# Two large tiles for v instead of three, and the last batch's v in the buffers of q and k

## The chip, the cores and the metric

The kernel runs on one core of one Trainium2 chip. The metric is the device time of one execution in microseconds (us). The kernel before took 256.08 us, the median of 3 runs (256.04 to 256.36).

## The reference

Two stages are computed for 4 batches of 6400 rows with 256 channels. The first is a cross-covariance attention: q and k are normalised along the rows, s = kn^T qn is a 256 x 256 matrix per batch, a is its softmax, and the result is v a. The second is a mixture of adapters: a gate picks 2 of 8 experts for each row and adds their low-rank (16) updates.

```python
qn = q / (np.linalg.norm(q, axis=1, keepdims=True) + 1e-06)
kn = k / (np.linalg.norm(k, axis=1, keepdims=True) + 1e-06)
s = kn.transpose(0, 2, 1) @ qn / tau
a = softmax(s)                      # over the last axis
x = (v @ a).reshape(25600, 256)
logits = x @ w_gate                 # 8 experts
topk = the two largest logits       # w: their softmax
out = x + sum over the two experts e of w_e * ((x @ A[e]) @ B[e])
```

The statistics of a batch need all of its q and k; only then can the rows of its v be worked on. q, k and v are float32 in memory, 26.2 MB each, and so is the output.

## The kernel before, in words

The 6400 rows of a batch lie on 128 partitions, 50 rows on each. A *chunk* is one such row index on all partitions (128 x 256 elements), so a batch has 50 chunks of each of q, k and v. A *pair* is two chunks of v and the unit of the second half of the work: pairs 0 to 24 belong to batch 0, 25 to 49 to batch 1, 50 to 74 to batch 2, 75 to 99 to batch 3.

**Loads.** All loads but the first few go through GpSimd's queue (POOL, lines 148, 149 and 151), which turns float32 into bf16 on the way. q and k come in tiles of 10 chunks each (one tile holds both; four buffers), v in tiles of 18, 16 and 16 chunks per batch (`VP`, three buffers). The list `loads` is sorted by the pair at which each load is due; `load_more` issues them strictly in that order and stops at the first one whose buffer still has unused chunks. So a load that waits for its buffer holds up all loads behind it. Since transposes wait for the load that holds their chunks, a load is of use only when the whole of it has landed. Batch 0's v and the last tile of v come in smaller pieces.

**Batch 0 first.** A first loop runs over batch 0's q and k: squares (ScalarE and VectorE in turn, lines 241 and 243), the Gram matrix on TensorE (`gram`, line 251), and sums of squares (`norm`). Then `chain0` to `chain6` turn them into the softmax matrix and its product with the gate's weights and the first adapter matrices.

**The slot loop.** After that a loop goes through slots. In slot n TensorE transposes pair n of v (`transposes`, line 400), and works on earlier pairs: `z_gz` (line 506), `gz_t` (line 530), `y_mm` (line 522), `delta` (line 542), and ScalarE copies the result into a buffer `ys` (line 546). Every five pairs form a group, with logits (line 421), a gating chain on VectorE, and one output of 10 chunks (1.31 MB). Into the same slots the Gram matrix of the next batch is dealt: batch 1 in slots 0 to 20, batch 2 in 24 to 45, batch 3 in 49 to 67, each followed by its chain. Each engine executes its instructions in the order in which this loop writes them.

**Outputs.** There are nine `ys` buffers. A finished group is put on the list `unsent`, and `send` (line 563, issued by ScalarE) sends groups only while more than `keep` are held: 7 until slot 70, then one less every four slots. The last ten pairs go out in small pieces by SyncE (line 550).

Of the kernel before, what the change touches and what calls it, by code (L numbers as in the profile page):

```python
# [9 lines left out]
BF16 = mybir.dt.bfloat16  # L10
# [6 lines left out]
def kernel(  # L17
# [17 lines left out]
    B, N, C = q.shape  # L35
    P = 128
# [8 lines left out]
    PC = 10  # L45
    NPAIR = NC // 2
    NPT = B * NPAIR
    GRP = 5
    QKB, VB, YB = 4, 3, 9
    VP = [18, 16, 16]  # L50
    FIRST = 4
    DEFER = 7

    GRAM = {1: (0, 20), 2: (24, 45), 3: (49, 67)}
# [9 lines left out]
    v_pool = ctx.enter_context(tc.tile_pool(name="vp", bufs=VB))  # L64
# [19 lines left out]
    for b, (first, last) in GRAM.items():  # L84
        n = last - first + 1
        for c in range(NC):
            s = first + c * n // NC
# [4 lines left out]
    loads = []  # L92

    for s in range(NC // PC):
        o = FIRST if s == 0 else 0
# [1 line left out]
        for b in range(1, B):  # L97
            loads.append((qk_need[b, s], "qk", b, s, 0, [PC]))
    for b in range(B):
        for s, n in enumerate(VP):  # L100
            at = NPAIR * b + sum(VP[:s]) // 2 + 1
            if b == 0:

                loads.append((at, "v", b, s, 0, [n - 8]))
                loads.append((at + (n - 8) // 2, "v", b, s, n - 8, [8]))
            else:
                loads.append((at, "v", b, s, 0,
                              [8, 4, 4] if b == B - 1 and s == len(VP) - 1 else [n]))
    loads.sort(key=lambda x: x[0])
    tiles = {"qk": {}, "v": {}}  # L110
    left = {"qk": [], "v": []}
    bufs = {"qk": QKB, "v": VB}
    where = {}
    at_load = [0]

    def piece(kind, c):

        if kind == "qk":
            return divmod(c, PC)
        s = 0  # L120
        while c >= VP[s]:
            c -= VP[s]
            s += 1
        return s, c

    def used(kind, b, c, n):
        left[kind][where[kind, b, piece(kind, c)[0]]] -= n

    def load_more(limit=1000):

        while limit and at_load[0] < len(loads):
            _, kind, b, s, o, parts = loads[at_load[0]]
            if (kind, b, s) not in where:
                n = len(left[kind])
                if n >= bufs[kind] and left[kind][n - bufs[kind]]:
                    return
                where[kind, b, s] = n
                left[kind].append(PC if kind == "qk" else VP[s])
                if kind == "qk":
                    t = qk_pool.tile([P, 2, PC, C], BF16, tag="qk", name="qk")  # L140
                else:
                    t = v_pool.tile([P, max(VP), C], BF16, tag="v", name="vt")
                tiles[kind][b, s] = t
            t = tiles[kind][b, s]
            c0 = s * PC if kind == "qk" else sum(VP[:s])
            for m in parts:
                if kind == "qk":
                    nc.gpsimd.dma_start(t[:, 0, o:o + m, :], q_v[b, :, c0 + o:c0 + o + m, :])  # L148
                    nc.gpsimd.dma_start(t[:, 1, o:o + m, :], k_v[b, :, c0 + o:c0 + o + m, :])
                else:  # L150
                    nc.gpsimd.dma_start(t[:, o:o + m, :], v_v[b, :, c0 + o:c0 + o + m, :])  # L151
                o += m
            at_load[0] += 1
            limit -= 1
# [22 lines left out]
    for c in range(0, FIRST, 2):  # L177
        t = tiles["qk"][0, 0]
# [54 lines left out]
    def square(b, c, eng):  # L233

        s, o = divmod(c, PC)
        t = tiles["qk"][b, s]
        sq = sq_pool.tile([P, 2, 2, C], BF16, tag="sq", name="sq")
        sqs[b, c] = sq
        src = t[:, :, o:o + 2, :]
        if eng == "act":  # L240
            nc.scalar.activation(sq, src, ACT.Square)  # L241
        else:
            nc.vector.tensor_tensor(out=sq, in0=src, in1=src, op=OP.mult)  # L243
# [137 lines left out]
    pr = {}  # L381
    free_banks = [False]
    unsent = []

    LAST = {NPT - 9: 4, NPT - 7: 4, NPT - 6: 2, NPT - 4: 4, NPT - 3: 2, NPT - 2: 2, NPT - 1: 2}

    def transposes(g, eng):

        b, p = divmod(g, NPAIR)
        gr = groups[g]  # L390
        if "vT" not in gr:
            gr["vT"] = vt_pool.tile([P, CC, 2 * GRP, P], BF16, tag="vT", name="vT")
        s, o = piece("v", 2 * p)
        vt = tiles["v"][b, s]
        full = ps_t.tile([P, 512], FP32, tag="pt", name="vT_ps")
        pt = full[:, 0:256].bitcast(BF16).rearrange("p (c t) -> p c t", c=CC)
        i = 0
        for sc in range(2):
            for ic in range(CC):
                nc.tensor.matmul(pt[:, ic, sc * P:(sc + 1) * P],  # L400
                                 vt[:, o + sc, ic * P:(ic + 1) * P], ident,
                                 is_transpose=True, start=(i == 0), stop=(i == 3))
                i += 1
        used("v", b, 2 * p, 2)
        w = 2 * (g - gr["f"])
        dst = gr["vT"][:, :, w:w + 2, :]
        src = pt.rearrange("p c (s t) -> p c s t", s=2)
        if eng == "act":
            nc.scalar.copy(dst, src)  # L409
        else:  # L410
            nc.vector.tensor_copy(dst, src)  # L411
        gr["full"] = full
        pr[g] = {"vT": dst, "w": w}
# [82 lines left out]
    def z_gz(u):  # L496
        b = u // NPAIR
        r, gr = pr[u], groups[u]

        banks = [(ps_z, "zg"), (ps_z, "zg"), (ps_acc, "acc"), (ps_nrm, "nrm")]  # L500
        pool, tag = banks[u % 4 if free_banks[0] else 0]
        zg = pool.tile([P, 512], FP32, tag=tag, name="zg")
        z = zg[:, 0:256].rearrange("p (s d) -> p s d", s=2)
        for sc in range(2):
            for ic in range(CC):
                nc.tensor.matmul(z[:, sc, :], r["vT"][:, ic, sc, :], st[b]["wa"][:, ic, E:E + ER],  # L506
                                 start=(sc == 0 and ic == 0), stop=(sc == 1 and ic == 1),
                                 skip_group_check=True)
        gz = work.tile([P, 2, ER], BF16, tag="gz", name="gz")
        nc.vector.tensor_tensor(  # L510
            out=gz.rearrange("p c (e r) -> p c e r", e=E),
            in0=z.rearrange("p c (e r) -> p c e r", e=E),
            in1=gr["gate"][:, r["w"]:r["w"] + 2, :].to_broadcast([P, 2, E, R]), op=OP.mult)
        r["gz"], r["zg"] = gz, zg
# [41 lines left out]
    def send(keep):  # L556


        eng = nc.scalar
        while len(unsent) > keep:  # L560
            gr = unsent.pop(0)
            c0, n = 2 * (gr["f"] - gr["b"] * NPAIR), 2 * gr["n"]
            eng.dma_start(out_v[gr["b"], :, c0:c0 + n, :], gr["ys"][:, 0:n, :])
# [49 lines left out]
    slot = 0  # L613
    zq, dq = None, None
    while nz < NPT or zq is not None or dq is not None:

        behind = nz + GRP < min(slot, NPT) and groups[nz + GRP]["ready"]
        items = [] if behind else todo.get(slot, [])
        h = (len(items) + 1) // 2
        f, us, fb = (None, 0.0, 0) if behind else at_chain.get(slot, (None, 0.0, 0))  # L620
        free_banks[0] = slot > GRAM[B - 1][1] + 4
        load_more()
        for b, c in items:
            if c % 2 == 0:
                square(b, c, "act")
        if f in (chain0, chain1, chain2, chain3):
            f(fb)
        u = None
        if nz < min(slot, NPT) and groups[nz]["ready"]:
            u = nz  # L630
            nz += 1
            z_gz(u)
        if zq is not None:
            gz_t(zq, "act" if slot >= NPT else "dve")
        gram_part(items[:h])
        if dq is not None:
            y_mm(dq)
        if slot < NPT and not behind:
            transposes(slot, "dve" if items or f is chain3 else "act")
        if dq is not None:  # L640
            delta(dq)
        dq, zq = zq, u
        send(max(0, min(DEFER, DEFER - (slot - GRAM[B - 1][1]) // 4)))
        if behind:
            deal(0.3)
            continue
        if 0 < slot <= NPT and slot - 1 == groups[slot - 1]["f"] + groups[slot - 1]["n"] - 1:
            logits(groups[slot - 1])
            ops = gating(groups[slot - 1])
            credit[0] -= ops[0][0]  # L650
            ops[0][1]()
            micro += ops[1:]
        gram_part(items[h:])
        if f in (chain4, chain5, chain6):
            f(fb)
        if items:
            deal(max(0.8 - us, 0.6))
        elif slot < NPT:
            deal(max(0.65 - us, 0.4))
        else:  # L660
            deal(0.5)
        slot += 1
# [35 lines left out]
```

## Time and profile before

| what | value |
|---|---|
| median of 3 runs | 256.08 us (256.04 to 256.36) |
| the profiled execution's own time | 255.97 us |
| its span, from the first to the last event in the profile | 254.2 us |
| TensorE (PE) busy | 220.1 us, 87% of the span |
| ScalarE (ACT) busy | 176.7 us, 70% |
| VectorE (DVE) busy | 155.4 us, 61% |
| GpSimd (POOL) busy | 32.6 us, 13% |
| loads through POOL's queue | 38.80 MB written in bf16, 59 issues |
| outputs by ScalarE, 1280 KB each | 18 issues, median 12.8 us from issue to landing |
| last output issued | 246.8 us |

The profile numbers lines by the file of its kernel (L400 is line 400), and times from the start of the span. A view in order of time has the start, the duration, the engine and line, the operation with its result and operands, and in brackets how long the engine stood idle just before and what ended that. In the view of the page's 40 slices each digit is the busy share of a slice of 6.4 us in tenths, and the row GB/s is what the transfers moved, counted in bytes as written: for a load that is half of what is read. A row of the view by stretches has the stretch, its length, the busy time and the number of instructions of PE, PEld (the weight loads), DVE, ACT and POOL, and then the TensorE clock that was granted, the share of the transfer engines and GB/s. A row of waits has the total, the number of times and the longest. A row of DMA issues has the queue, the number, the size as written and the median from issue to landing.

### The profile page before, as it was taken

Reading aid. Unit: us, or ns where it says so; the run is one execution under the profiler, and the core shown is the slowest. Engines: PE = TensorE matmul, PEld = TensorE weight load, DVE = VectorE, ACT = ScalarE, POOL = GpSimd, SP = SyncE. Lnnn points to the kernel's source line nnn. Section 1 sums busy time; section 2 is a strip of 40 time slices with the busy share of each in tenths; the row PEclk is TensorE's granted clock in tenths of the full one; section 3 lists DMA queues with packets and bytes.
Section 4 is the critical chain, followed back from the end, with each engine's and each line's share of the span. In section 5 each row is a group of like instructions: output and inputs, shape, how many; then the busy total and the mean of one; then the engine's idle time right before and its main releaser. Section 6 shows DMA issues by size and latency. Waiting matters only on the chain.

```text
span 254.2 us, 7429 instructions
## 1 busy us (share of the span) xinstructions
PE 220.1 (87%) x3122; PEld 190.0 (75%) x3122; DVE 155.4 (61%) x583; ACT 176.7 (70%) x291; POOL 32.6 (13%) x67
## 2 busy tenths in 40 slices
PE   0787793895999999999999999999899899999960
PEld 0444471785998878989999779989797799999950
DVE  1334534363758669676776786848487776777730
ACT  2434353876687798877977978788766878877860
POOL 8031221112111202020110102000000200000000
PEclk9999998697999999999999999999999999999997
DMA  7999999999999999999999999999999999999995
GB/s 210 230 211 218 209 217 214 213 214 217 213 212 216 224 206 218 215 211 219 214 218 213 210 292 239 249 285 288 247 294 285 399 319 352 408 421 425 423 416 233
DMA packets 12849, 66.80 MB, mean 263 GB/s; under 512 B 1552, under 2 KB 1808, under 8 KB 9488
## 3 DMA queue, kind: packets, MB, share of 16 engines
q0 software_dynamic: 8496, 38.80, 74.9%
q10 hardware_dynamic: 2592, 23.59, 22.5%
q1 hardware_dynamic: 1728, 3.94, 4.3%
q8 instruction: 24, 0.39, 0.6%
q14 instruction: 9, 0.07, 0.1%
HBM read 78.91 MB, written 26.21 MB: 414 GB/s over the span
## 4 chain that ended last, share of the span: by engine, by line
PE 48%; DMA 36%; DVE 7%; ACT 3%; issue 2%; POOL 1%; DVEq 0%; ACTq 0%; POOLq 0%
DMA qk<-in_k_dram 31%; PE y_ps L522 12%; PE acc L251 8%; PE zg L506 6%; PE y_ps L542 6%; PE vT_ps L400 5%; DMA out_dram<-ys 5%; PE zg L530 3%; PE vT_ps L421 3%; PE nrm L268 3%; ACT sq L241 2%; DVE gz L510 2%; ACT ys L546 1%; POOL qk L148 1%; DVE lm L456 1%
## 5 line engine op out<-in xcount | busy, mean ns | idle before, releaser
L241 ACT ACTIVATE sq<-qk 128x1024 bf16<-128x1024 bf16 x87 | 89.6, 1054 | 20.9 <-DMA qk<-in_k_dram 18.7
L251 PE MATMUL acc<-qk 128*128 128x256 bf16 x400 | 73.8, 285 | 16.1 <-DMA qk<-in_k_dram 9.6
L546 ACT COPY ys<-y_ps 128x512 f32<-128x512 f32 x100 | 58.8, 588 | 21.5 <-PE y_ps L542 18.4
L522 PE MATMUL y_ps<-a_bf,vT 128*128 128x256 bf16 x400 | 59.9, 272 | 0.4 <-ACT ys L546 0.4
L251 PEld LDWEIGHTS <-qk 128*128 128x128 bf16 x400 | 34.3, 101 | 26.2 <-DMA qk<-in_k_dram 12.3
L510 DVE TENSOR_TENSOR gz<-zg,gate 128x256 bf16<-128x256 f32 x100 | 41.7, 418 | 14.3 <-PE zg L506 13.0
L411 DVE COPY vT<-vT_ps 128x512 bf16<-128x512 bf16 x63 | 26.7, 423 | 28.0 <-PE vT_ps L400 27.4
L268 PEld LDWEIGHTS <-sq 128*128 128x128 bf16 x600 | 36.0, 97 | 6.7 <-ACT sq L241 2.8
L400 PE MATMUL vT_ps<-ident,vt 128*128 128x128 bf16 x400 | 39.5, 222 | 0.9 <-DMA vt<-in_v_dram 0.7
L506 PE MATMUL zg<-wa_sb,vT 128*128 128x128 bf16 x400 | 38.5, 219 | 1.2 <-DVE gzT L536 1.1
L542 PE MATMUL y_ps<-ball_sb,gzT 128*128 128x256 bf16 x200 | 38.2, 273 | 0.0
L268 PE MATMUL nrm<-ones_bf,sq 128*128 128x1 bf16 x600 | 35.6, 164 | 1.2 <-ACT sq L241 1.2
L522 PEld LDWEIGHTS <-vT 128*128 128x128 bf16 x400 | 33.5, 97 | 3.2 <-issue 0.5
L400 PEld LDWEIGHTS <-vt 128*128 128x128 bf16 x400 | 30.0, 99 | 3.8 <-DMA vt<-in_v_dram 1.4
L409 ACT COPY vT<-vT_ps 128x512 bf16<-128x512 bf16 x37 | 21.7, 587 | 10.2 <-PE vT_ps L400 8.9
L530 PE MATMUL zg<-ident,gz 128*128 128x128 bf16 x200 | 27.7, 220 | 1.1 <-DVE gz L510 0.6
L506 PEld LDWEIGHTS <-vT 128*128 128x128 bf16 x400 | 26.0, 97 | 3.3 <-issue 2.2
L536 DVE COPY gzT<-zg 128x256 bf16<-128x256 bf16 x90 | 25.3, 281 | 0.0
L148 POOL DMA_DIRECT2D qk<-in_q_dram x21 | 11.4, 544 | 89.2 <-ACT sq L241 23.4
L243 DVE TENSOR_TENSOR sq<-qk 128x1024 bf16<-128x1024 bf16 x13 | 9.1, 700 | 19.6 <-DMA qk<-in_k_dram 12.4
L151 POOL DMA_DIRECT2D vt<-in_v_dram x17 | 9.1, 535 | 66.2 <-PE y_ps L542 49.4
L530 PEld LDWEIGHTS <-gz 128*128 128x128 bf16 x200 | 15.2, 98 | 2.9 <-DVE gz L510 2.5
(68 smaller groups left out, 188.6 us busy)
## 6 DMA issues: line engine op xcount, KB each, us to landing
out_dram<-ys ACTq DMA_DIRECT2D x18, 1280.0 KB, 12.8
qk<-in_q_dram POOLq DMA_DIRECT2D x18, 640.0 KB, 21.3
qk<-in_k_dram POOLq DMA_DIRECT2D x18, 640.0 KB, 23.4
vt<-in_v_dram POOLq DMA_DIRECT2D x5, 1024.0 KB, 28.2
vt<-in_v_dram POOLq DMA_DIRECT2D x3, 1152.0 KB, 26.4
vt<-in_v_dram POOLq DMA_DIRECT2D x6, 512.0 KB, 22.1
out_dram<-ys SPq DMA_DIRECT2D x3, 512.0 KB, 8.7
out_dram<-ys SPq DMA_DIRECT2D x4, 256.0 KB, 7.1
```

What stands on the lines that cost most here:

```text
L241: nc.scalar.activation(sq, src, ACT.Square)
L251: nc.tensor.matmul(acc[b][:, ic, :], t[:, 1, o, ic * P:(ic + 1) * P], t[:, 0, o, :], start=(c == 0 and ic == 0), stop=(c == NC - 1), skip_ ...
L268: nc.tensor.matmul(nrm[b][:, j:j + 1], sq[:, w, c % 2, ic * P:(ic + 1) * P], ones_bf[:, 0:1], start=(c == 0 and j == 0), stop=(c == NC - 1 ...
L400: nc.tensor.matmul(pt[:, ic, sc * P:(sc + 1) * P], vt[:, o + sc, ic * P:(ic + 1) * P], ident, is_transpose=True, start=(i == 0), stop=(i = ...
L411: nc.vector.tensor_copy(dst, src)
L506: nc.tensor.matmul(z[:, sc, :], r["vT"][:, ic, sc, :], st[b]["wa"][:, ic, E:E + ER], start=(sc == 0 and ic == 0), stop=(sc == 1 and ic == ...
L510: nc.vector.tensor_tensor(out=gz.rearrange("p c (e r) -> p c e r", e=E), in0=z.rearrange("p c (e r) -> p c e r", e=E), in1=gr["gate"][:, r ...
L522: nc.tensor.matmul(y[:, sc, :], r["vT"][:, ic, sc, :], st[b]["a"][:, ic, :], start=(sc == 0 and ic == 0), stop=False, skip_group_check=True)
L530: nc.tensor.matmul(gt[:, sc, :], r["gz"][:, sc, :], ident, is_transpose=True, start=(sc == 0), stop=(sc == 1))
L536: nc.vector.tensor_copy(gzT, gt)
L542: nc.tensor.matmul(r["y"][:, sc, :], r["gzT"][:, sc, :], ball_sb, start=False, stop=(sc == 1), skip_group_check=True)
L546: nc.scalar.copy(gr["ys"][:, r["w"]:r["w"] + 2, :], r["y"])
```

## The change

v of batches 0 to 2 comes in tiles of 26 and 24 chunks, with two buffers instead of three. v of batch 3 comes in tiles of 20, 20 and 10 chunks, which take their turn in the four buffers of q and k. Batch 0's two tiles are loaded in pieces of 10, 8, 8 and 8, 8, 8 chunks; every other tile of v is one load. The number of groups held back no longer falls from a fixed slot on, but from the last slot at which some load has not been issued, by one every three slots instead of four. In the order that results, the second tile of v of batch 2 is issued behind the last tile of q and k, as the third one was before, and the last batch's three tiles are issued in slots 57, 61 and 64 (before: 59, 67 and 75).

```diff
-    QKB, VB, YB = 4, 3, 9
-    VP = [18, 16, 16]
+    QKB, VB, YB = 4, 2, 9
+
+    VP = [[26, 24]] * 3 + [[20, 20, 10]]
...
-        for s, n in enumerate(VP):
-            at = NPAIR * b + sum(VP[:s]) // 2 + 1
+        for s, n in enumerate(VP[b]):
+            at = NPAIR * b + sum(VP[b][:s]) // 2 + 1
             if b == 0:
 
-                loads.append((at, "v", b, s, 0, [n - 8]))
+                loads.append((at, "v", b, s, 0, [n - 16]))
+                loads.append((at + (n - 16) // 2, "v", b, s, n - 16, [8]))
                 loads.append((at + (n - 8) // 2, "v", b, s, n - 8, [8]))
             else:
-                loads.append((at, "v", b, s, 0,
-                              [8, 4, 4] if b == B - 1 and s == len(VP) - 1 else [n]))
+                loads.append((at, "v", b, s, 0, [n]))
...
+    def ring(kind, b):
+        return "qk" if b == B - 1 else kind
...
             if (kind, b, s) not in where:
-                n = len(left[kind])
-                if n >= bufs[kind] and left[kind][n - bufs[kind]]:
+                r = ring(kind, b)
+                n = len(left[r])
+                if n >= bufs[r] and left[r][n - bufs[r]]:
                     return
                 where[kind, b, s] = n
-                left[kind].append(PC if kind == "qk" else VP[s])
-                if kind == "qk":
+                left[r].append(PC if kind == "qk" else VP[b][s])
+                if r == "qk":
                     t = qk_pool.tile([P, 2, PC, C], BF16, tag="qk", name="qk")
+                    if kind == "v":
+                        t = t.rearrange("p w c d -> p (w c) d")
                 else:
-                    t = v_pool.tile([P, max(VP), C], BF16, tag="v", name="vt")
+                    t = v_pool.tile([P, max(VP[b]), C], BF16, tag="v", name="vt")
...
-        send(max(0, min(DEFER, DEFER - (slot - GRAM[B - 1][1]) // 4)))
+        if at_load[0] < len(loads):
+            all_loads[0] = slot
+        send(max(0, DEFER - (slot - all_loads[0]) // 3))
```

## The prediction

> **What bounds the kernel now.** I read the 40 slices first, then the chain of waits in order of time, then the waits of the load queue (POOL), then TensorE (PE) around the loads that the change moves.
>
> ```profile
> span 254.2 us, 7429 instructions
> ...
> DMA  7999999999999999999999999999999999999995
> GB/s 210 230 211 218 209 217 214 213 214 217 213 212 216 224 206 218 215 211 219 214 218 213 210 292 239 249 285 288 247 294 285 399 319 352 408 421 425 423 416 233
> ...
> HBM read 78.91 MB, written 26.21 MB: 414 GB/s over the span
> ```
>
> The transfer engines are full from the second slice to the last but one. A load reads float32 and writes bf16, so 215 GB/s in the row is 430 GB/s at HBM; outputs alone run at 421 to 425. Both halves thus move some 424 GB/s of HBM bytes, and 78.91 + 26.21 = 105.1 MB at 424 GB/s is 248 us of a span of 254.2. Moving a load earlier cannot make these bytes fewer. Earlier loads only push outputs later; a gain is limited to what is ragged at the two ends.
>
> ```profile
> 152.95 27.28 DMA qk<-in_k_dram
> 180.33 1.68 ACT sq L241 x2
> 182.00 13.15 DMA out_dram<-ys
> 195.23 0.60 ACT ys L546
> 195.87 0.60 PE y_ps L522 x4
> ```
>
> The chain of waits has two transfers late in the run: the last tile of q and k, which lands at 180.2, and an output that frees a result buffer at 195.15. From there to the last copy at 246.18 it is PE and the gating chain. In the ten-microsecond windows PE is busy 9.3 to 10 of 10 from 60 us to 240. So two things are nearly full at once: DMA and PE. Time that PE loses to a wait is not made up later; it moves the last output.
>
> ```profile
> POOL vt L151 <- PE y_ps L542: 49.4, 5, 18.5
> ```
>
> This is the wait the change works on: POOL stands 49.4 us in five waits for a free v tile. While it stands, the transfer engines stay full (the DMA row), so these 49.4 us are not on the path.
>
> **The change, part by part.** The order of instructions on PE, DVE and ScalarE is the same in both kernels but for the places of 18 output issues and the tile that the last batch's transposes read. The load queue changes: v of batches 1 and 2 comes as 26 + 24 chunks instead of 18 + 16 + 16. Loads are issued in order, and transposes wait for the whole load of their tile.
>
> *Fewer issues.* 55 loads instead of 59, at 0.53 us of POOL: 2.1 us less on an engine that is busy 13%. Worth nothing.
>
> *First tile of v of batch 1.* It keeps its place in the queue but has 26 chunks, not 18. Its load:
>
> ```profile
> 68.99 0.53 POOL L151 DMA_DIRECT2D vt<-in_v_dram  x1 [2.81 <-PE acc L251]
> ```
>
> The DMA issues of that window give 24.6 us to landing, so 93.6. The first transposes on it (pair 25) start at 94.08, 0.5 us later. Eight chunks more are 524 KB in bf16, at 215 GB/s 2.4 us: landing at 96.0, a new PE wait of 1.9 us. Behind it in PE's order stand pair 25's transposes, the logits of pairs 20 to 24, the gram of batch 2 and all that follows.
>
> *Second tile of v of batch 2: the step that decides.* In both kernels the last load of batch 2's v is issued right behind the last tile of q and k. Ahead of it stand, in both, all of q and k and the rest of v of batches 0 to 2: the same 542 chunks are done when it lands.
>
> ```profile
> 152.95 0.54 POOL L149 DMA_DIRECT2D qk<-in_k_dram  x1
> 153.47 0.55 POOL L151 DMA_DIRECT2D vt<-in_v_dram  x1
> ```
> ```profile
> vt<-in_v_dram POOLq DMA_DIRECT2D x1, 1024.0 KB, 31.8
> ```
> ```profile
> 178.11 0.39 PE L400 MATMUL vT_ps<-ident,vt 128*128 128x128 bf16 x4
> 180.27 0.39 PE L251 MATMUL acc<-qk 128*128 128x256 bf16 x2 [0.91 <-DMA qk<-in_k_dram]
> 187.73 0.39 PE L400 MATMUL vT_ps<-ident,vt 128*128 128x128 bf16 x4
> ```
>
> The first view is POOL's timeline, the second the issues of that window: 153.47 + 31.8 = 185.3. In the kernel before, this load holds chunks 34 to 49, first wanted by pair 67 at 187.73, so it comes 2.4 us early. After the change it holds chunks 26 to 49, first wanted by pair 63, at 178.11. PE will stand at pair 63 until the same landing. The output issued at 182.00 shared the engines for the last 3.3 us at most (some 45% of the bytes, by 188 against 236 GB/s at HBM in the mixed stretches, worked out from the packets), which is 1.5 us; it is issued after pair 64 and so no longer competes. I take half: landing at 184.5, pair 63 later by **6.4 us** (bounds 5.7 and, if an earlier output sent late lies in its way instead, 8.7). The 1.9 us at pair 25 is not added: the landing hardly depends on when PE gets there.
>
> *Waits that go.* The 0.91 us at 180.27 vanishes, since PE reaches that tile later: **-0.9**. The 0.37 us at 169.24 for v goes too, but lies ahead of pair 63 and is swallowed there. The wait for a result buffer at 195.23 cost PE 0.6 us; the output that it waits for is issued after pair 64 and is late by the same amount, so I take 0 (bounds -0.6 and 0).
>
> *The clock.* A gap on PE has a second price here:
>
> ```profile
> 59.89 0.61 PE L251 MATMUL acc<-qk 128*128 128x256 bf16 x2 [2.67 <-DMA qk<-in_k_dram]
> ```
> ```profile
> 60.00:63.20 3.20, 3.20 (x34) 2.77 (x34) 1.05 (x3) 3.20 (x4) 0.87 (x2) 0.51 1.06 216
> 64.00:70.00 6.00, 6.00 (x108) 5.64 (x107) 4.54 (x20) 3.67 (x6) 1.06 (x2) 1.00 1.05 213
> ```
>
> After a gap of 2.7 us the granted clock was 0.51 for 3.4 us, then 1.00 again; after one of 3.0 us near 42 us it was half for 6.8 us. Gaps of 1.6 us and less left no mark. The gap at pair 63 is over 4 us, in a stretch where PE has no slack. Half clock for 3.4 us loses 1.7 us; bounds 0 and 3.4 (6.8 us of it). I take the row nearest to it in the chain, **+1.7**.
>
> The Trainium skill (TensorE: Matmul & The Clock Gate, Part 1) puts the fall to half rate behind an idle window of about 3.4 us. By that rule the wait at pair 25 costs no clock and that at pair 63 does, as I reckon; the trace is harsher, since 2.7 us were enough.
>
> *The output schedule and the last batch's tiles.* The last batch's v goes into q and k buffers and is issued after pairs 56, 60 and 63 instead of 58, 66 and 74; outputs leave 3 to 6 pairs earlier from pair 66 on. No transposes of the last batch waited for v before, so nothing is gained. What it does: the loads are done sooner, the outputs held back are sent sooner, and with PE late the engines run dry near the end.
>
> *Sum.* 6.4 - 0.9 + 1.7 = 7.2 us on PE's path. The last output was issued at 246.8 (out_dram view); it goes out at 254.0. Before it landed 6.3 us later behind a full queue; the bytes that are left are done near 251.6, so it finds a short queue. The nearest row is a load of 512 KB with nothing ahead (3.8 us); bounds 3.8 and 6.3, I take 3.8. From landing to the end the kernel before has 254.2 - 253.1 = 1.1. End 258.9, 4.7 us over 254.2. The profiled execution took 255.97, 1.77 over its span and 0.1 below the median 256.08. Forecast **260.7 us**.
>
> **Rivals.**
>
> *Not slower: the queues share by rows.* A load of 24 chunks has rows of 24 KB against 10 KB of an output; if each engine takes a row from each queue in turn, loads get 70% and not 55%. The 24 chunks (3.15 MB) then pass in 10.6 instead of 13.5 us. It decides from 5.6 us earlier on (landing by 179.7, with pair 25's wait in front): that needs nearly all of the bandwidth. Then the path shifts by 1.9 - 0.4 - 0.9 = 0.6 us, hidden in the full queue at the end: 256.0, at best 255.2 when pair 25 is on time too. Against it: mixed stretches with rows of 10 and of 18 chunks show the same split (222 to 195, 234 to 186). Chance 0.08.
>
> *Not slower: a fixed cost per load.* If each load costs its queue 2.8 us beside its bytes, the two loads fewer ahead of that tile bring it 5.6 us sooner: again 256.0. Against it: 60 to 70 us, with loads of 8 and 10 chunks, moves 214 GB/s, 90 to 100 us, with larger ones, 210. Chance 0.06. The Trainium skill (DMA: Bandwidth & Descriptors, Rules for kernel authors) asks for 1 MiB and more per DMA, which speaks for this change; those two rows show no such gain while the queue is never empty.
>
> *Pair 63 waits, the clock stays.* 260.7 - 1.7 = 259.0; down to 257 with the short bounds. For it: the gate's window has its own phase. Chance 0.2.
>
> *Worse.* The half clock holds 6.8 us, or the later landing: 262.4 to 264.7. Chance 0.06.
>
> **How the numbers follow.** The forecast's own case has 0.60, with 258.5 to 263. Low 256.8 leaves out the two rivals that are not slower (0.14), high 263.4 most of the rest. 0.2% (0.5 us) is about what a measurement of this kernel can tell from no change. The 0.14 lie at 255.2 to 256.5: faster 0.06, same 0.08; all else is slower, 0.86.
>
> **What would show it.** In the profile after: PE idle at pair 63 (L408 there) by 4 to 7 us until a v load lands near 185, named as released by DMA vt; a shorter one at pair 25 near 94; a granted clock of half behind the first; no wait at 195 that is longer than before; the DMA row below 9 in slices after 235 us; the last v landing before 210 instead of 218. Wrong would be: pair 63's tile landing by 180, or PE making up the gap, which would put slack on PE where I see none.

## The result, and the profile after

The changed kernel takes 258.99 us (median of 5 runs, 258.76 to 259.32) against 256.15 for the kernel before on the same chip: a ratio of 1.0117, with a 95% interval of 1.0106 to 1.0128. It is 2.8 us slower. The forecast was 260.7, slower, with a range from 256.8 to 263.4. The profiled execution took 258.91 us with a span of 257.1, 2.9 over the span before. Of the four executions of before_later, below, one took 363.38 us at a granted clock of 0.571 and is left out.

The page of the kernel after, the span, the clock and the transfer rows in 40 slices (of 6.4 us each):

```profile
span 257.1 us, 7425 instructions
...
PEclk9999997697999997999999999999679999999999
DMA  7999999999999999999999999999999999999696
GB/s 211 228 215 215 209 216 214 214 215 214 215 213 213 222 210 214 215 231 201 213 221 214 210 274 257 241 297 261 268 218 300 381 426 425 425 420 393 249 384 230
...
HBM read 78.91 MB, written 26.21 MB: 409 GB/s over the span
```

The bytes are the same. The transfer engines are full as before up to slice 37 and run short in slice 38: 249 GB/s, where the kernel before had 423. The clock row has new lows in slice 16 and in slices 29 and 30.

The POOL wait that the change works on did shrink, from 49.4 us to 18.8:

```profile
POOL vt L158 <- PE y_ps L550: 18.8, 3, 10.9
```

Nothing came of it on the path. What happened instead stands in the timeline of PE, at the first transposes on the two tiles that grew (pairs 25 and 63):

```profile
95.82 0.40 PE L408 MATMUL vT_ps<-ident,vt 128*128 128x128 bf16 x4 [1.81 <-DMA vt<-in_v_dram]
184.09 0.61 PE L408 MATMUL vT_ps<-ident,vt 128*128 128x128 bf16 x4 [3.72 <-DMA vt<-in_v_dram]
```

and in the chain that ended last, which now runs through the load that pair 63 waits for:

```profile
156.09 27.95 DMA vt<-in_v_dram
184.09 0.61 PE vT_ps L408 x4
```

The same chain also runs through the load for pair 25, for 26.41 us from 69.36 on. It says what was waited for in turn, not what each wait is worth; that is left to the experiments.

The stretches of the kernel after show the granted clock behind the two gaps (third value from the end; the first row is pair 63, the last pair 25), and, from 238 us on, transfer engines with too little to do (second from the end):

```profile
184.00:189.20 5.20, 5.11 (x42) 4.18 (x43) 1.47 (x4) 2.58 (x4) 0.53 (x1) 0.50 1.05 225
238.00:243.00 5.00, 5.00 (x80) 4.68 (x79) 4.01 (x20) 4.17 (x10) 0.00 (x0) 1.00 0.74 304
243.00:250.00 7.00, 7.00 (x84) 6.37 (x82) 4.95 (x24) 6.01 (x17) 0.00 (x0) 1.00 0.82 332
97.00:100.40 3.40, 3.40 (x41) 3.15 (x39) 2.32 (x10) 0.45 (x1) 0.00 (x0) 0.50 1.04 212
```

Since the compute engines execute the same instructions in the same order, each pair can be compared with itself. PE's lateness against the kernel before, from the start of each pair's transposes in the two traces: -0.2 us at pair 24, +1.7 at pair 25, +2.6 from pair 27 on (PE runs at half clock from 97.0 to 100.4), +2.1 at pair 60 (the old wait at 169.24 is gone), **+6.0 at pair 63**, +6.7 at 64, +7.2 at 66, and +6.9 from 74 to the last copy at 253.13 instead of 246.18. The end of the kernel moved by only 2.9.

### The profile page after: what moved, and what is told of

Same layout as the page of the kernel before. It is cut to its first block, busy times and chain, and to the rows that moved or that the text cites. A ratio compares the mean times of both kernels' runs of the same rounds, so it can differ in the third digit from the quotient of the medians.

```text
span 257.1 us, 7425 instructions
## 1 busy us (share of the span) xinstructions
PE 223.2 (87%) x3122; PEld 192.9 (75%) x3122; DVE 155.5 (60%) x583; ACT 176.8 (69%) x291; POOL 30.4 (12%) x63
## 4 chain that ended last, share of the span: by engine, by line
PE 47%; DMA 41%; DVE 6%; issue 2%; ACT 2%; POOL 1%; DVEq 0%; POOLq 0%; ACTq 0%
DMA vt<-in_v_dram 21%; DMA qk<-in_k_dram 20%; PE y_ps L530 11%; PE acc L258 8%; PE zg L514 6%; PE vT_ps L408 6%; PE y_ps L550 6%; PE zg L538 4%; PE vT_ps L429 3%; PE nrm L275 2%; DVE gz L518 1%; ACT sq L248 1%; DVE e L460 1%; DVE lg L452 1%; POOL qk L155 1%
## 5 line engine op out<-in xcount | busy, mean ns | idle before, releaser
L258 PE MATMUL acc<-qk 128*128 128x256 bf16 x400 | 75.1, 289 | 15.1 <-DMA qk<-in_k_dram 8.7
L554 ACT COPY ys<-y_ps 128x512 f32<-128x512 f32 x100 | 58.7, 587 | 26.6 <-PE y_ps L550 24.4
L258 PEld LDWEIGHTS <-qk 128*128 128x128 bf16 x400 | 34.9, 103 | 25.3 <-DMA qk<-in_k_dram 11.2
L275 PEld LDWEIGHTS <-sq 128*128 128x128 bf16 x600 | 36.7, 99 | 7.0 <-ACT sq L248 2.5
L514 PE MATMUL zg<-wa_sb,vT 128*128 128x128 bf16 x400 | 39.2, 221 | 1.1 <-DVE gzT L544 1.1
L408 PE MATMUL vT_ps<-ident,vt 128*128 128x128 bf16 x300 | 30.4, 226 | 5.9 <-DMA vt<-in_v_dram 5.5
L408 PEld LDWEIGHTS <-vt 128*128 128x128 bf16 x300 | 22.7, 101 | 8.5 <-DMA vt<-in_v_dram 6.3
L550 PEld LDWEIGHTS <-gzT 128*128 128x128 bf16 x200 | 16.3, 99 | 0.4
## 6 DMA issues: line engine op xcount, KB each, us to landing
qk<-in_v_dram POOLq DMA_DIRECT2D x2, 1280.0 KB, 26.4
```

Source lines behind the costliest of these rows:

```text
L258: nc.tensor.matmul(acc[b][:, ic, :], t[:, 1, o, ic * P:(ic + 1) * P], t[:, 0, o, :], start=(c == 0 and ic == 0), stop=(c == NC - 1), skip_ ...
L275: nc.tensor.matmul(nrm[b][:, j:j + 1], sq[:, w, c % 2, ic * P:(ic + 1) * P], ones_bf[:, 0:1], start=(c == 0 and j == 0), stop=(c == NC - 1 ...
L408: nc.tensor.matmul(pt[:, ic, sc * P:(sc + 1) * P], vt[:, o + sc, ic * P:(ic + 1) * P], ident, is_transpose=True, start=(i == 0), stop=(i = ...
L550: nc.tensor.matmul(r["y"][:, sc, :], r["gzT"][:, sc, :], ball_sb, start=False, stop=(sc == 1), skip_group_check=True)
L554: nc.scalar.copy(gr["ys"][:, r["w"]:r["w"] + 2, :], r["y"])
```

## The experiments

Two theories stood against each other. *Mine*: the landing of batch 2's second v tile sets how late PE is; the late PE then starves the transfer engines at the end. *Rivals*: the waits add up one by one; or the other half of the change (the last batch's buffers and the sooner outputs) costs the time; or the fewer buffers do. All edits but those of the last two runs are made to the changed kernel; in the diffs `-` is the kernel that is edited.

**split_25.** The tile of pair 25 in two loads.

```diff
-                loads.append((at, "v", b, s, 0, [n]))
+                loads.append((at, "v", b, s, 0, {(1, 0): [18, 8]}.get((b, s), [n])))
```

> The first v tile of batch 1 is loaded as 18 + 8 chunks in two loads at the same place in the queue; all else is as changed. Theory (the landing of batch 2's second v tile sets how late PE is, whatever came before): the wait at pair 25 (1.8 us) and the half clock behind it go, the wait at pair 63 grows from 3.7 to about 6 us and still ends near 184, the last copy stays near 253, the time at 258.9 within 0.5. Rival (each wait adds its own part): the 2.6 us by which PE was late behind pair 25 come off, 256.3 to 256.6.

Measured: 258.98 us, ratio to the kernel before 1.0122 (1.0102 to 1.0142). PE's timeline:

```profile
102.30 0.39 PE L258 MATMUL acc<-qk 128*128 128x256 bf16 x2 [0.93 <-DMA qk<-in_k_dram]
184.36 0.61 PE L408 MATMUL vT_ps<-ident,vt 128*128 128x128 bf16 x4 [4.31 <-DMA vt<-in_v_dram]
```

The wait and the half clock at pair 25 are gone and the time is the same; at pair 63 PE waits until the same 184. But this run tells less than it was meant to. PE is late by 1.2 us at pair 25 even so (the half clock near 42 us lasted 10.2 us in this execution, 6.8 in that of the kernel before), and by 2.3 us from pair 28 on: the eight chunks still stand ahead of batch 2's second tile of q and k, and that one is late now, which I had not foreseen. PE reaches pair 63 only 0.3 us sooner than in the changed kernel (180.05 instead of 180.37) and goes on 0.3 us later. So the landing sets when PE goes on, over this small difference; no run brought PE to pair 63 on time, and the rival that the waits add up is refuted no further than that.

**split_63.** The tile of pair 63 in two loads.

```diff
-                loads.append((at, "v", b, s, 0, [n]))
+                loads.append((at, "v", b, s, 0, {(2, 1): [8, 16]}.get((b, s), [n])))
```

> Only the second v tile of batch 2 is loaded as 8 + 16 chunks, in two loads at the same place. Theory: the 8 chunks land some 8 us sooner, before pair 63 wants them, so the wait at pair 63 and its half clock go; PE stays about 2 us late from pair 25, which the full output queue hides for the most part: 256.1 to 256.8. Rival (the last batch's tiles in the buffers of q and k and the sooner outputs cost the time): 258 and more.

Measured: 255.71 us, ratio 0.9989 (0.9980 to 0.9999). The whole loss is gone, and the time lies 0.4 us below the expected range. The DMA issues at 155.6 us, the part of 8 chunks:

```profile
vt<-in_v_dram POOLq DMA_DIRECT2D x1, 512.0 KB, 22.2
```

It lands at 155.58 + 22.2 = 177.8, before pair 63 wants it at 179.7. PE is 2.1 us late from pair 28 to pair 55 here too (the changed kernel: 2.6), 1.6 of it from before pair 25, where half clock near 61 us lasted 6.8 us instead of 3.4. Lateness of this size ahead of pair 63 costs nothing by itself. PE is also 2.0 us late at its last copy, 0.5 of it from before pair 66 and the rest from a wait for a result buffer, and the time does not show it.

**split_all.** All four tiles of batches 1 and 2 in two loads.

```diff
-                loads.append((at, "v", b, s, 0, [n]))
+                loads.append((at, "v", b, s, 0, {(1, 0): [18, 8], (1, 1): [8, 16], (2, 0): [18, 8], (2, 1): [8, 16]}.get((b, s), [n])))
```

> All four v tiles of batches 1 and 2 are loaded in two parts (18 + 8 and 8 + 16), same order, same buffers. Theory: no wait on v longer than before; the transfer engines are full as before and PE is some 1 us earlier than before at the end; 255.2 to 256.1. Rival (fewer v buffers or the output schedule cost something by themselves): 257 and more.

Measured: 255.88 us, ratio 0.9997 (0.9987 to 1.0007): no difference from the kernel before. The time is as expected, PE is not: it ends 2.3 us later than before, not earlier. It is on time up to pair 27 and then waits for the tile of q and k that split_25 pointed at:

```profile
102.03 0.39 PE L258 MATMUL acc<-qk 128*128 128x256 bf16 x2 [1.94 <-DMA qk<-in_k_dram]
```

Near pair 60 ScalarE also waits 3.0 us for a result buffer (1.8 in the kernel before).

**fill_63.** PE is given work in the gap, to see what the fall of its clock costs.

```diff
+        if g == 63:
+            for _ in range(36):
+                nc.tensor.matmul(full[:, 0:256], ident, ball_sb, start=True, stop=True)
```

> 36 matmuls of 256 columns with no result that is used are put on PE just ahead of pair 63's transposes, so that PE works through most of the 3.7 us in which it would wait. They are work added, and the load lands when it lands. Theory (the fall to half clock behind the gap costs some 2.5 us): the granted clock stays at 1.0 behind pair 63, PE is about 4.5 instead of 7 us late at the end, the time falls to 256.5 to 257.2. Rival (the half clock costs nothing, PE is not the limit there): 258.9 or, with the added work, more.

Measured: 257.92 us, ratio 1.0076 (1.0061 to 1.0091). PE's timeline and the stretch behind it:

```profile
180.08 4.09 PE L407 MATMUL vT_ps<-ball_sb,ident 128*128 128x256 bf16 x36
184.77 0.40 PE L411 MATMUL vT_ps<-ident,vt 128*128 128x128 bf16 x4 [0.59 <-DMA vt<-in_v_dram]
```
```profile
184.00:189.20 5.20, 4.61 (x70) 4.16 (x69) 2.10 (x6) 3.78 (x5) 0.53 (x1) 1.00 1.04 225
```

In the same 5.2 us PE does 70 matmuls at full clock, 42 at half. The transposes start 0.7 us later than in the changed kernel, and by pair 66 PE is 5.6 us late instead of 7.2. So the half clock costs some 2.3 us there (1.6 and the 0.7). But the time fell by some 1 us, not by 2: the chain of this kernel shows what took the rest.

```profile
187.60 13.48 DMA out_dram<-ys
201.16 0.59 ACT ys L557
```

Pair 60's copy waits for a result buffer until that output has landed. In the changed kernel the same copy starts at 201.44, 0.3 us later. Past it PE is 6.5 us late against 6.9. Most of the clock's price was covered by this wait, which my expectation had left out. The 0.4 us that remain on PE are less than the 1 us by which the time fell; the rest is not explained.

**last_only.** One half of the change alone: `VP = [[18, 16, 16]] * 3 + [[20, 20, 10]]`, three v buffers, batch 0's v in its old pieces; the last batch's buffers and `send` as changed.

> One half of the change alone: v of batches 0 to 2 in tiles of 18, 16 and 16 with three buffers as before, the last batch's v in tiles of 20, 20 and 10 in buffers of q and k, outputs held back until the last load is issued. Theory (this half neither costs nor brings anything, since the transfer engines are full either way and no transposes of the last batch waited for v): 255.5 to 256.3. Rival (sooner loads and outputs are worth something once the late tile of batch 2 is out of the way): 255.0 or less. Second rival (this half carries the loss): 257 and more.

Measured: 255.69 us, ratio 0.9992 (0.9983 to 1.0002). The half with the buffers of q and k and the sooner outputs costs nothing; a gain is not shown. ScalarE's wait for a result buffer does grow, from 1.8 to 2.6 us, and PE's last copy is 0.7 us later, within what the end of this section finds to be hidden.

**tiles_only.** The other half alone.

```diff
-    VP = [[26, 24]] * 3 + [[20, 20, 10]]
+    VP = [[26, 24]] * 4
...
-                loads.append((at, "v", b, s, 0, [n]))
+                loads.append((at, "v", b, s, 0, [8, 8, 8] if (b, s) == (B - 1, 1) else [n]))
...
-        return "qk" if b == B - 1 else kind
+        return kind
...
-        send(max(0, DEFER - (slot - all_loads[0]) // 3))
+        send(max(0, min(DEFER, DEFER - (slot - GRAM[B - 1][1]) // 4)))
```

> The other half alone: tiles of 26 and 24 chunks with two buffers for all four batches (the last tile in three loads of 8), outputs as before the change. Theory (the loss is the late second tile of batch 2): pair 63 waits until some 184, half clock behind it, 258.6 to 259.6. Rival (the loss needs the other half, whose outputs leave sooner): 257 or less.

Measured: 263.83 us, ratio 1.0317 (1.0291 to 1.0343), 4 to 5 us worse than expected. The wait at pair 63 is there until 184.1, as the theory has it, and PE ends 5.6 us late, less than in the changed kernel. What makes the kernel slower still is the transfer engines. The page's row, POOL's timeline and the stretch:

```profile
DMA  7999999999999999999999999999956899999995
```
```profile
205.27 1.59 POOL L158 DMA_DIRECT2D vt<-in_v_dram  x3 [26.63 <-PE y_ps L550]
```
```profile
190.00:200.00 10.00, 10.00 (x174) 9.24 (x173) 7.93 (x32) 7.70 (x16) 0.00 (x0) 1.00 0.49 189
```

With two large buffers POOL stands 26.6 us until the last tile's buffer is free, while the old rule still holds seven groups of outputs back. The engines are then half idle for 10 us around 195 in a kernel that they bound, and the time lost there is not made up. So the two halves belong together: without the second, the first costs 7.9 us, with it 2.8.

**split_63_defer6.** split_63 with `DEFER = 6` instead of 7, an attempt to do better than both.

> The changed kernel with batch 2's second v tile loaded as 8 + 16 chunks, and one group of outputs fewer held back (6 instead of 7), so that each result buffer is free sooner. Theory (the bytes bound the time now, PE may be 2 us early or late): the wait for a result buffer (2.6 us in the kernel with 7) goes, PE ends 1.5 to 2 us sooner, the time stays at 255.3 to 255.8. Rival (PE's lateness still costs): 254.5 or less. Second rival (an output sent sooner holds up the last tile of q and k): 256.5 and more.

Measured: 258.34 us, ratio 1.0090 (1.0069 to 1.0110): my theory missed, and the time is that of the second rival, with the load of v behind the last tile of q and k held up. The part of 8 chunks (DMA issues at 155.6 us) and PE:

```profile
vt<-in_v_dram POOLq DMA_DIRECT2D x1, 512.0 KB, 27.5
```
```profile
183.14 0.61 PE L408 MATMUL vT_ps<-ident,vt 128*128 128x128 bf16 x4 [3.26 <-DMA vt<-in_v_dram]
```

One output more, 1.31 MB, is sent ahead of this load. At 424 GB/s that is 3.1 us; the load lands 5.3 us later (183.1, not 177.8), of which 2.2 are not explained, and the wait at pair 63 is back, with the half clock behind it. split_63 has only 1.9 us in hand there.

**before_late and before_later.** The kernel before, loads and outputs untouched, with PE made late by work that is not used: 36 matmuls (72 in the second) ahead of pair 76.

```diff
+        if g == 76:
+            for _ in range(36):
+                nc.tensor.matmul(full[:, 0:256], ident, ball_sb, start=True, stop=True)
```

> The kernel before, with 36 matmuls of 256 columns whose result is not used put on PE ahead of pair 76's transposes: 3.9 us of work added in a stretch without slack, no gap, the clock at 1.0. Theory (a full queue of outputs hides about 4 us of PE's lateness): PE's last copy is 3.7 to 3.9 us later and the time only 0.2 to 0.8 above before, 256.2 to 256.8. Rival (as the prediction's sum has it, about 2.5 us are hidden): 257.3 to 257.6. Second rival (none is hidden): 259.8.

> The kernel before with 72 instead of 36 unused matmuls ahead of pair 76's transposes, 7.8 us of work; loads and outputs are untouched. Theory (the changed kernel's loss is PE's lateness alone, of which the queue of outputs hides about 4 us): PE's last copy 6.5 to 7.3 us later, as in the changed kernel, and the time 258.5 to 259.3, the changed kernel's own. Rival (the changed loads and outputs cost something beside PE's lateness): 258 or less here.

Measured: 255.96 us, ratio 1.0002 (0.9993 to 1.0012), with PE's last copy 3.0 us later (less than the 3.7 to 3.9 expected); and 259.14 us, ratio 1.0127 (1.0106 to 1.0147), with PE's last copy 7.0 us later. So 3.0 us of lateness cost nothing, and 7.0 us cost what the changed kernel costs, with not one load or output edited. PE's lateness alone is enough for the loss. The times from issue to landing of the outputs in the kernel before (the shortest, 6.3 us, is the last output's), and the last two outputs in the kernel with 72:

```profile
DMA to landing us min/median/max: 6.3/12.0/15.4
```
```profile
out_dram<-ys SPq DMA_DIRECT2D x2, 256.0 KB, 2.5
```

The last output lands 2.5 us after issue, in the kernel before 6.3 us, behind a full queue. The difference, 3.8 us, is what was hidden: 7.0 - 3.8 = 3.2, the difference of the two spans (257.4 and 254.2). In before_late the last outputs took 3.2 us: 3.1 of these 3.8 us were used up there, by a PE 3.0 us late.

## Why the prediction was right, and what was mis-sized

The mechanism holds at the step that decides; the end was forecast at 258.9 and measured at 257.1, so the sum was 1.8 us too high, and two smaller steps were wrong (the clock at pair 25, and what stands behind that load in the queue).

- *DMA and PE both full, earlier loads worth nothing*: right. The wait on POOL fell by 30 us, and for last_only and split_all the intervals hold 1, so no difference from the kernel before is shown. (One reading was off: PE's least busy window, from 140 to 150 us, has 9.1 of 10, not 9.3. Nothing rests on it.)
- *Pair 25*: landing forecast 96.0, measured 69.36 + 26.4 = 95.8; wait forecast 1.9, measured 1.81. That it does not add to the loss rests on the arrivals in the next point, since no run had PE on time there. That it costs no clock was wrong: the clock fell for 3.4 us behind it. And the prediction overlooked that the eight chunks more also delay the tile of q and k behind them, for which PE waits 1.9 us in split_all.
- *Pair 63*: landing forecast 184.5, measured 184.0 (156.09 + 27.9); PE later by 6.0 instead of 6.4. That the place in the queue and nothing else decides is seen in the other kernels: the 542nd chunk lands between 184.0 and 185.5 in the kernel before, the changed one, split_63, tiles_only and last_only, and only one more output ahead of it moves it (188.0 in split_63_defer6). PE is done with what stands ahead of pair 63 at 180.4 us in the changed kernel, 180.1 in split_25 and 179.8 in tiles_only, and goes on at 184.1, 184.4 and 184.1: when it goes on does not follow when it came.
- *The wait at 180.27 gone*: forecast -0.9; from fill_63, pair 63 to 64, -1.1.
- *The clock*: forecast 1.7 (one stretch of 3.4 us), measured 2.3: it was the longer stretch of 6.8 us, of which 5.1 lay behind the gap. In tiles_only the stretch behind the same wait lasted 3.4 us; which of the two it would be, the prediction had no means to tell. The Trainium skill (TensorE: Matmul & The Clock Gate, Part 1) says that the clock falls after an idle window of some 3.4 us. The trace does not agree: the clock fell 2.0 us after PE had stopped at pair 63 (180.4 and 182.4), and behind the gap of 1.8 us at pair 25.
- *The wait for a result buffer*: forecast 0, measured -0.3.
- *PE's path*: forecast 7.2, measured 6.0 - 1.1 + 2.3 - 0.3 = 6.9. Last output issued at 253.7, forecast 254.0.
- *The term that was mis-sized*: the landing of the last output. I took 3.8 us, the row of a load of 512 KB with nothing ahead, as the lower bound; two pieces of 256 KB took 2.4:

```profile
out_dram<-ys SPq DMA_DIRECT2D x2, 256.0 KB, 2.4
```

That is 1.4 of the 1.8 us; the path has 0.3 more. Put in another way, the queue of outputs hides 4 us of PE's lateness, not 2.5; the runs give 6.9 - 2.9 = 4.0 in the changed kernel, 7.0 - 3.2 = 3.8 in before_later, and 3.0 us cost nothing in before_late.
- *The signs named*: the wait at pair 63 is there, with 3.7 us a little short of the 4 to 7 named; half clock behind it, the row below 9 behind 235 us, and the last v landing at 186.1 + 19.4 = 205.5 (forecast before 210) are all there.
- *The rivals*: a fixed cost per load or a larger share for long rows would have brought pair 63's tile sooner; it came 0.5 us sooner than I reckoned, where 5 were needed. The measured 258.99 us is the very time of the third rival, *pair 63 waits, the clock stays* (259.0), but not its mechanism: the clock was at 0.50 behind pair 63, and fill_63 shows that it cost PE 2.3 us. The time alone could not have told the two apart; a last output that landed 1.4 us sooner than reckoned happened to offset the clock's price. The condition of the rival *worse*, half clock for 6.8 us, did come true, and its time of 262.4 and more did not.

What stays open is a gain. split_63 is the best of all at 0.9989; its interval ends at 0.9999, so it is at most a fifth of a per cent below the kernel before, and last_only with 0.9992 cannot be told from it. Every kernel that keeps the transfer engines full ends between 255.7 and 256.2. What would shorten the start and the end of the transfers was not tried.

## What to carry to other kernels

When a load gets larger at the same place in a queue, its first bytes become available only with its last: find which earlier consumer now waits for it, and compare that consumer's time with the landing before the change. Keep the large buffer and load it in two parts if the first consumer is early. When two resources are nearly full, measure how much lateness of one the queue of the other hides (here 4 us), because up to there a wait costs nothing (3.0 us cost nothing here) and beyond it counts (7.0 us cost 3.2).

## What the runs showed of the hardware that I had not expected

A gap on PE of 1.8 us was followed by half clock for 3.4 us (97.0 to 100.4 in the kernel after), while gaps of 1.6 us in the kernel before were not; in split_63 a shorter wait at the same place left the clock at 1.0. The stretches of half clock lasted 3.4, 6.8 or 10.2 us, the last near 42 us in split_25, fill_63 and last_only, where the kernel before had 6.8.

The length of a gap is not what decides. In each of the eleven traces the granted clock changes only at times that lie whole multiples of 3.41 us apart. Take the intervals of 3.41 us on this grid with the clock at 1.0, from 12.5 us to the end of PE's work: where PE stood idle for 1.75 us or more in all, the next interval was at half clock, 30 times of 30; where it stood for 1.6 us or less, the next was at 1.0 every time. So it matters where a gap falls. The 1.8 us at pair 25 lay within one interval. In split_all 1.9 us near 101 were cut into 1.2 and 0.7, and the clock stayed. The gap at pair 63 put 2.0 us into one interval and 1.7 into the next, and half clock held for two; in tiles_only a gap of 4.3 us filled one interval and left 0.5 and 0.4 on its sides, and half clock held for one. This is read from the traces, with the ends of matmuls as they are modelled there; no run moved a gap on purpose.

And 24 chunks in one load went through the full queue at the same pace as 16, or 8 and 16: the chunk with the same number landed within 1.5 us in five kernels.
